# A two-layer decode kernel on one core: longer rows for some weights, a smaller last piece of wo, and the gate half of the last SwiGLU done ahead of the up half

## The chip, the cores and the metric

The kernel runs on one core of a Trainium2 chip. The core has five engines that run their own instruction streams: TensorE (PE in the profile, its weight loads PEld), VectorE (DVE), ScalarE (ACT), GpSimd (POOL) and SyncE (SP), which here only issues DMA transfers. All transfers of the core are split over 16 DMA engines. The metric is device time in microseconds; the time before is a median of several executions, and one more execution was profiled.

## The reference

Two equal layers, each an attention block on a cached window and a SwiGLU block, on a single token of width 640:

```python
W = min(4096, max(256, Sk // 4))            # 4096 of the 32768 cached rows
q = (x @ wq).reshape(B, Sq, 32, 192)        # wq: 640 x 6144
k = k_cache[:, :, Sk - W:, :]               # 32 heads, 4096 x 192 each
v = v_cache[:, :, Sk - W:, :]
p = softmax(q @ k^T * 192 ** -0.5)
att = (p @ v).reshape(B, Sq, 6144) @ wo     # wo: 6144 x 640
ffn = (silu(x @ w1) * (x @ w3)) @ w2        # w1, w3: 640 x 1536, w2: 1536 x 640

x = x + att(layernorm(x));  x = x + ffn(layernorm(x))    # layer 0
x = x + att(layernorm(x));  x = x + ffn(layernorm(x))    # layer 1
```

Both layers use the same weights and the same caches. Everything is bf16 in memory.

## The kernel before, in words

**Pages.** SBUF holds an arena of 16 slots (`NSLOT`), each 128 partitions by 6144 bf16 values (`PGW`), which is 1536 KB. One head's K window or V window fills one slot; so does one fifth of wq. wo comes as pieces of 9 chunks (a chunk is 128 rows of wo, 640 values on each partition), w1 and w3 as four of their five chunks of 1536 values, and a page `fc` holds the fifth chunk of w1, the fifth of w3 and the first four of the 12 chunks of w2. `fd` holds the next five chunks of w2. Three chunks of wo (`wo5`) and three of w2 (`keep`) stay in SBUF from layer 0 to layer 1, as do 14 heads of K (`RETAIN`); one of these is parked in PSUM (`stash`), so 13 slots are taken up around the change of layer and three are free.

**What sets the order.** `loads` (lines 163 to 198) is the list of all transfers in the order in which the data are used. `refill` (lines 200 to 212) takes from its head as long as a slot is free, and issues the transfers on SyncE; `done` frees a slot after its last use and calls `refill`. The instruction order on each engine is the order in which the Python code emits them, since nearly all are pinned by `pin`. The framework gives SyncE's transfers eight semaphores in turn: an issue waits for the landing of the transfer eight before it, and for the last reader of the slot that it overwrites. A transfer spreads over the 16 DMA engines by rows; each partition's row is one packet, 12288 B for a full page.

**One layer.** `attention` normalizes x, forms q (`qproj`: per wq chunk 12 products of 512 columns, then copies that lay q out as weights), and then runs over the 32 heads: for each K page two 32x32-block transposes on DVE (line 300), 12 score products, softmax per four heads, and six heads later 16 products with the V page. `wo_proj` (line 397) multiplies the chunks of wo in order, two products of 320 columns a chunk with a single column of weights, the three kept chunks last. `y_to_residual` adds the result to x, which lies spread over partitions in `xsq`.

**The ffn** (line 417). Layernorm gives `xs`. Four column strips of TensorE work side by side, so a chunk of w1 or w3 is four products of 384 columns: 16 for gate (page `fa`), 16 for up (`fb`), 4 and 4 for the fifth chunks (`fc`). Then both halves are copied to bf16, gate by ACT (line 444) and up by DVE (line 445), turned by three small products each to 12 values on each partition (line 449), and silu(gate) x up is made by one ACT and five DVE operations on 12 columns (lines 451 to 460), which give `htd`. In layer 0 twelve chunks of w2 are multiplied and added to the residual. In layer 1 `last_rows` (line 477) adds the residual by ten f32 product records (five products with the residual as weights; an f32 product has two records) into the same PSUM tile `f_ps`, then 48 products of `htd` with w2, four strips of 160 columns a chunk, the kept chunks seventh to ninth; DVE copies the row (line 489), and SyncE writes it out.

Layer 1's last transfers are split so that the last one is small: w2's chunks 4 to 8 come as 1280, 1280 and 640 columns.

Of the kernel before, what the change touches and what calls it, by code (L numbers as in the profile page):

```python
# [47 lines left out]
def kernel(  # L48
# [82 lines left out]
    zero = cst.tile([P, 32], BF16, name="zero")  # L131
# [15 lines left out]
    wq_v = A_wq.rearrange("(p c) n -> c p n", c=NCH)  # L147
# [5 lines left out]
    ORDER = ((3, 2, 1, 0), (1, 0, 2, 3))  # L153

# [7 lines left out]

    for layer in range(2):
        for c in range(NCH):
            loads.append((("q", layer, c), [(0, PGW, wq_v[c])]))
        for i in range(H + LEAD):
            for kind, g, cache in (("v", i - LEAD, A_v_cache), ("k", i, A_k_cache)):
# [3 lines left out]
                if kind == "k" and layer == 1 and h in RETAIN:  # L171
                    if h == STASH:
                        loads.append((("k", 1, h), []))
                    continue
                loads.append(((kind, layer, h),
                              [(0, PGW, cache[0, h, S0:SK, :].rearrange("(p t) d -> p (t d)", p=P))]))
        for w in range(6):
            parts = []
            for at, ci in enumerate(wo_order(layer)[9 * w:9 * w + 9]):
                blk, e = ORDER[layer][ci // 12], ci % 12  # L180
                if parts and parts[-1][2] == blk and parts[-1][3] + parts[-1][1] == e:
                    parts[-1][1] += 1
                else:
                    parts.append([at, 1, blk, e])
            parts = [(640 * at, 640 * n, wo_v[blk][:, 640 * e:640 * (e + n)]) for at, n, blk, e in parts]
            if w < 5:
                loads.append((("o", layer, w), parts))
            elif layer == 0:
                assert len(parts) == 1 and parts[0][1] == 1920
                loads.append((None, [(wo5[:], parts[0][2])]))  # L190
        loads.append((("fa", layer), [(0, PGW, w1_v[:, 0:PGW])]))
        loads.append((("fb", layer), [(0, PGW, w3_v[:, 0:PGW])]))
        loads.append((("fc", layer), [(0, 1536, w1_v[:, PGW:]), (1536, 1536, w3_v[:, PGW:]),
                                      (3072, 2560, w2_v[:, 0:2560])]))
        fd = [(0, 3200)] if layer == 0 else [(0, 1280), (1280, 1280), (2560, 640)]
        loads.append((("fd", layer), [(o, n, w2_v[:, 2560 + o:2560 + o + n]) for o, n in fd]))
        if layer == 0:
            loads.append((None, [(keep[:], w2_v[:, 5760:7680])]))

    def refill():  # L200
        while loads and (free or loads[0][0] is None):
            key, parts = loads.pop(0)
            if key is None:
                for dst, src in parts:
                    pin(nc.sync.dma_start(out=dst, in_=src))
                continue
            s = free.pop(0)
            home[key] = s
            for off, n, src in parts:
                pin(nc.sync.dma_start(out=arena[:, s * PGW + off:s * PGW + off + n], in_=src))  # L210
# [11 lines left out]
    def page(key):  # L222
        return arena[:, home[key] * PGW:home[key] * PGW + PGW]

    def done(key):
        free.append(home.pop(key))
        refill()
# [169 lines left out]
    def wo_proj(layer):  # L397
        y_ps = y_open("y_ps")
        for w in range(6):
            pg = page(("o", layer, w)) if w < 5 else wo5  # L400
            for cc, ci in enumerate(wo_order(layer)[9 * w:9 * w + 9]):
                n = 9 * w + cc
# [5 lines left out]
            if w < 5:  # L408
                done(("o", layer, w))
        y_to_residual(y_ps)  # L410

    def w2_chunk(layer, fcx):
        if fcx >= 9:
            return keep, 640 * (fcx - 9)
        return (page(("fc", layer)), 3072 + 640 * fcx) if fcx < 4 else (page(("fd", layer)), 640 * (fcx - 4))

    def ffn(layer):
# [15 lines left out]
        for ps, kind, c0, c1, off in ((g_ps, "fa", 0, 4, 0), (u_ps, "fb", 0, 4, 0),  # L433
                                      (g_ps, "fc", 4, 5, 0), (u_ps, "fc", 4, 5, 1536)):
            pg = page((kind, layer))
# [5 lines left out]
            if kind != "fc":  # L441
                done((kind, layer))
        gu = w20.rearrange("p (g n) -> p g n", g=2)
        pin(nc.scalar.copy(out=gu[:, 0, :], in_=g_ps[:, 0:384]))
        pin(nc.vector.tensor_copy(out=gu[:, 1, :], in_=u_ps[:, 0:384]))
        gt_ps = m_ps[:, 0:24].rearrange("p (g k j) -> p g k j", g=2, k=3)
        for gi in range(2):
            for k in range(3):
                mm(gt_ps[:, gi, k, :], lhsT=gu[:, gi, k:384:3], rhs=sel4[:], start=True, stop=True)
        ex = sml.tile([P, 12], F32, tag="ex", name="ex")  # L450
        pin(nc.scalar.activation(out=ex[:], in_=gt_ps[:, 0, :, :].rearrange("p k j -> p (k j)"), func=ACTF.Exp,
                                 scale=-1.0))
        ut = sml.tile([P, 12], F32, tag="ut", name="ut")
        pin(nc.vector.tensor_copy(out=ut[:], in_=gt_ps[:, 1, :, :].rearrange("p k j -> p (k j)")))
        gut = sml.tile([P, 12], F32, tag="gut", name="gut")
        pin(nc.vector.tensor_tensor(out=gut[:], in0=gt_ps[:, 0, :, :].rearrange("p k j -> p (k j)"), in1=ut[:],
                                    op=ALU.mult))
        pin(nc.vector.tensor_scalar_add(out=ex[:], in0=ex[:], scalar1=1.0))
        pin(nc.vector.reciprocal(out=ex[:], in_=ex[:]))
        pin(nc.vector.tensor_tensor(out=_ap(htd[:], 0, P, 0, [[1, 3], [3, 4]]),  # L460
                                    in0=gut[:].rearrange("p (k j) -> p k j", k=3),
# [100 lines left out]
```

## Time and profile before

| What | Value |
|---|---|
| Time, median of 3 runs | 528.83 us (528.5 to 529.74) |
| Profiled execution, its own time | 528.32 us |
| Span of its trace, first to last instruction | 526.6 us |
| Read from HBM | 221.58 MB, 421 GB/s over the span |
| PE busy | 275.0 us (52%), 2403 records |
| DVE busy | 256.4 us (49%) |
| ACT, POOL busy | 62.5 us, 16.2 us |
| Mean granted TensorE clock | 0.716 of full speed |

The page gives an engine's busy time as a share of the span, then the span in 40 slices with a digit for the busy tenths, the DMA queues, the chain of waits that ended last, and the costliest groups of instructions. In the timeline a row is a run of like instructions: start, length, engine, line, what is written and read, and in brackets the idle time before it with what ended it. The view by windows gives busy time and number of instructions for PE, PEld, DVE, ACT and POOL in each stretch, then the granted clock, the DMA share and GB/s. Every time in the text is counted from the span's start.

### The profile page before, as it was taken

To read this page: it belongs to the slowest core of one execution; us is meant where nothing else is said; L and a number is where in the kernel's file an instruction comes from. 1 tells how busy PE (TensorE), PEld (TensorE's weight loads), DVE (VectorE), ACT (ScalarE), POOL (GpSimd) and SP (SyncE) were. 2 spreads that over 40 slices of the span, in tenths; PEclk is the share of its full clock that TensorE was granted. 3 is DMA by queue.
4 is the path that set the end of the run, shared out by engine and by line. 5 is a ranking of instruction groups with operands and counts; after the bars stand their busy time and mean duration, and the time that the engine had idled before them with its cause. 6 is when DMAs were issued, how large, how long until landed. Compare 5 with 4: busy or idle time off the path is not lost.

```text
span 526.6 us, 5978 instructions
## 1 busy us (share of the span) xinstructions
PE 275.0 (52%) x2403; PEld 112.6 (21%) x2403; DVE 256.4 (49%) x393; ACT 62.5 (12%) x192; POOL 16.2 (3%) x74
## 2 busy tenths in 40 slices
PE   2344644472655644455545555687254756345455
PEld 1111211131222221122112112233022322112113
DVE  1199676556657475654002139531475645753001
ACT  1002020110102020112001002022111120202000
POOL 4000000000000000000000000000000000001000
PEclk9997968666756776586556558988677886686557
DMA  8999999999999999999999999999999999999995
GB/s 349 429 430 433 426 428 427 433 432 427 427 428 432 432 426 429 428 432 423 419 431 422 427 428 427 420 431 427 428 428 431 429 428 429 429 431 428 424 432 242
DMA packets 22355, 221.97 MB, mean 421 GB/s; under 512 B 2616, under 2 KB 2744, under 8 KB 5176
## 3 DMA queue, kind: packets, MB, share of 16 engines
q1 hardware_dynamic: 22184, 221.59, 99.3%
q8 instruction: 19, 0.31, 0.2%
q14 instruction: 8, 0.07, 0.0%
q10 hardware_dynamic: 144, 0.00, 0.0%
HBM read 221.58 MB, written 0.00 MB: 421 GB/s over the span
## 4 chain that ended last, share of the span: by engine, by line
DMA 85%; PE 7%; DVE 5%; issue 1%; ACT 1%; SPq 1%; DVEq 0%; ACTq 0%
DMA arena<-in_A_k_cache_dram 51%; DMA arena<-in_A_v_cache_dram 16%; DMA arena<-in_A_wo_dram 9%; DMA arena<-in_B_w_dram 6%; DMA arena<-in_A_wq_dram 3%; DVE arena L300 3%; PE s_ps L80 3%; PE o_ps L80 2%; PE y_ps L80 1%; SPq L210 1%; PE q_ps L80 1%; PE u_ps L80 0%; PE pss L80 0%; ACT w L337 0%; DVE t L322 0%
## 5 line engine op out<-in xcount | busy, mean ns | idle before, releaser
L80 PE MATMUL s_ps<-arena,wst 128*32 128x512 bf16 x768 | 153.7, 512 | 171.3 <-DVE arena L300 84.5
L300 DVE STREAM_TRANSPOSE arena<-arena 128x1536 uint32<-128x1536 uint32 x100 | 171.2, 1754 | 75.0 <-DMA arena<-in_A_k_cache_dram 74.6
L80 PE MATMUL o_ps<-arena,ptm 128*8 128x384 bf16 (+1 forms) x1024 | 113.5, 421 | 12.9 <-DMA arena<-in_A_v_cache_dram 12.9
L80 PEld LDWEIGHTS <-wst 128*32 128x32 bf16 x768 | 53.1, 115 | 256.2 <-issue 227.1
L80 PEld LDWEIGHTS <-ptm 128*8 128x8 bf16 (+1 forms) x1024 | 40.0, 99 | 49.9 <-issue 40.3
L332 ACT ACTIVATE tb<-m 32x16 f32<-32x16 f32 x16 | 3.4, 214 | 280.4 <-DVE m L329 280.4
L350 ACT COPY ptm<-w 32x64 bf16<-32x64 bf16 x80 | 23.6, 295 | 42.5 <-PE o_ps L80 39.3
L80 PE MATMUL y_ps<-arena,otd 128*1 128x320 bf16 x180 | 16.9, 459 | 15.1 <-DMA arena<-in_A_wo_dram 15.1
L80 PE MATMUL q_ps<-arena,xs 128*32 128x512 bf16 x120 | 14.5, 624 | 17.3 <-DMA arena<-in_A_wq_dram 14.7
L383 DVE SCALAR_TENSOR_TENSOR w<-pss,rl,mask 64x192 bf16<-64x192 f32 x16 | 6.7, 417 | 32.2 <-PE pss L80 32.2
L282 POOL COPY wst<-qt_sb 32x24 bf16<-32x24 bf16 x30 | 8.4, 281 | 432.7 <-PE s_ps L80 313.8
L340 DVE STREAM_TRANSPOSE w<-w 64x512 bf16<-64x512 bf16 x16 | 11.3, 705 | 14.4 <-ACT w L337 14.4
L248 DVE CAST w<-y_ps 128x320 bf16<-128x320 f32 x3 | 1.5, 490 | 34.4 <-PE y_ps L80 34.4
L322 DVE TENSOR_REDUCE t<-s_ps 64x1 f32<-64x512 f32 x16 | 10.6, 663 | 12.2 <-PE s_ps L80 12.1
L274 DVE CAST qt_sb<-pss 32x192 bf16<-32x192 f32 x2 | 0.7, 346 | 31.2 <-PE pss L80 31.2
L350 DVE COPY ptm<-w 32x64 bf16<-32x64 bf16 x48 | 9.9, 207 | 10.8 <-PE o_ps L80 9.6
L80 PEld LDWEIGHTS <-xs 128*32 128x32 bf16 x200 | 7.2, 119 | 35.7 <-issue 26.1
L355 DVE RECIPROCAL rl<-pss 64x1 f32<-64x1 f32 x16 | 2.6, 166 | 22.2 <-PE pss L80 22.2
L80 PEld LDWEIGHTS <-otd 128*1 128x1 bf16 x192 | 6.4, 103 | 25.8 <-issue 21.7
L337 ACT ACTIVATE w<-s_ps,nbt 64x512 bf16<-64x512 f32 x16 | 10.9, 682 | 5.6 <-DVE nbt L334 5.6
L376 ACT CAST w<-o_ps 128x384 bf16<-128x384 f32 x16 | 7.7, 479 | 33.0 <-PE o_ps L80 23.7
L80 PE MATMUL pss<-w,sel 128*64 128x192 bf16 x32 | 6.3, 286 | 9.5 <-ACT w L376 6.4
(82 smaller groups left out, 111.8 us busy)
## 6 DMA issues: line engine op xcount, KB each, us to landing
arena<-in_A_v_cache_dram SPq DMA_DIRECT2D x64, 1536.0 KB, 29.2
arena<-in_A_k_cache_dram SPq DMA_DIRECT2D x50, 1536.0 KB, 29.2
arena<-in_A_wq_dram SPq DMA_DIRECT2D x10, 1536.0 KB, 9.3
arena<-in_A_wo_dram SPq DMA_DIRECT2D x6, 1440.0 KB, 15.3
arena<-in_B_w_dram SPq DMA_DIRECT2D x4, 1536.0 KB, 11.1
arena<-in_A_wo_dram SPq DMA_DIRECT2D x4, 960.0 KB, 16.8
arena<-in_A_wo_dram SPq DMA_DIRECT2D x4, 480.0 KB, 21.8
arena<-in_B_w_dram SPq DMA_DIRECT2D x4, 384.0 KB, 14.6
```

The lines of the kernel that those rows point to most:

```text
L80: return pin(nc.tensor.matmul(*a, **k))
L210: pin(nc.sync.dma_start(out=arena[:, s * PGW + off:s * PGW + off + n], in_=src))
L282: pin((engs[a].copy if engs[a] is nc.scalar else engs[a].tensor_copy)(out=dst, in_=src))
L300: pin(nc.vector.transpose(x[:, w * sp:w * (sp + 1)].bitcast(U32), x[:, w * sp:w * (sp + 1)].bitcast(U32)))
L322: pin(nc.vector.reduce_max(out=t0[:, 0:1], in_=s_ps[0:64, :], axis=AX.X))
L332: pin(nc.scalar.mul(out=tb[32:64, :].rearrange("p (a z) -> p a z", a=4)[:, :, 0:HB], in_=mb, mul=-SCALE))
L337: pin(nc.scalar.activation(out=e[:], in_=s_ps[0:64, :], func=ACTF.Exp, bias=nbt[:, 0:1], scale=SCALE, accum_out=l[:]))
L340: pin(nc.vector.transpose(et[:], e[:]))
L350: pin((eng.copy if eng is nc.scalar else eng.tensor_copy)(out=dst, in_=src))
L355: pin(nc.vector.reciprocal(out=rl[half], in_=rl_ps[half]))
L376: pin(nc.scalar.copy(out=o_sb[:, 0:384], in_=o_ps[:, 0:384]))
L383: pin(nc.vector.scalar_tensor_tensor(out=om, in0=ot_ps[half], scalar=rl[half], in1=mask[half].unsqueeze(2).broadcast_to([64, 16, 12]), op0 ...
```

## The change

- wq of layer 0 comes as one chunk, two and two in place of five single ones; a pair takes two neighbouring slots.
- wo of layer 1 comes in pieces of 12, 12, 12 and 9 chunks in place of five of 9; a piece of 12 takes two neighbouring slots and is one transfer of 1920 KB. The piece of 9 is two transfers of 6 and 3 chunks (960 and 480 KB). The kept three chunks are multiplied before that last piece. Before, the pieces crossed head blocks and made seven transfers; now there are five.
- w1 of layer 1 comes whole, five chunks in two neighbouring slots; w3 as four chunks and one; w2's first nine chunks as 3840, 1280 and 640 columns. Six transfers in place of eight. The kept w2 chunks are multiplied first.
- The gate half is copied, turned and put through silu by the new `gate()`, and up is multiplied in by a single operation at the end; `gut` and one copy go. In layer 1 `gate()` is emitted between the products with w3's four chunks and those with its fifth, so DVE's copy of up now stands behind it. In layer 0 `gate()` stands after that copy.
- `refill` looks for the first free slot whose neighbours are free where a load has several keys, and stops otherwise; `zero` is 64 wide in place of 32.

```diff
+    def slots(key, width):
+        return [key] + [key + (i,) for i in range(1, -(-width // PGW))]
...
+    def wo_units(layer):
+        order = wo_order(layer)
+        step = 9 if layer == 0 else 12
+        return [order[at:min(at + step, 45)] for at in range(0, 45, step)] + [order[45:]]
...
-        for c in range(NCH):
-            loads.append((("q", layer, c), [(0, PGW, wq_v[c])]))
+        for c0, c1 in ((0, 1), (1, 3), (3, 5)) if layer == 0 else [(c, c + 1) for c in range(NCH)]:
+            loads.append(([("q", layer, c) for c in range(c0, c1)],
+                          [(0, PGW * (c1 - c0), wq_r[:, PGW * c0:PGW * c1])]))
...
+            if layer == 1 and w + 2 == len(units):
+                (at, n, blk, e), = parts
+                parts = [[at, n - 3, blk, e], [at + n - 3, 3, blk, e + n - 3]]
...
+        rows = 4 if layer == 0 else 5
+        loads.append((slots(("fa", layer), 1536 * rows), [(0, 1536 * rows, w1_v[:, 0:1536 * rows])]))
+        loads.append(([("fb", layer)], [(0, PGW, w3_v[:, 0:PGW])]))
...
+        else:
+            loads.append(([("fc", layer)], [(0, 1536, w3_v[:, PGW:])]))
+            loads.append(([("fd", layer)], [(o, n, w2_v[:, o:o + n]) for o, n in ((0, 3840), (3840, 1280), (5120, 640))]))
...
+            n = len(keys)
+            at = [s for s in free if all(s + i in free for i in range(n))]
+            if not at:
+                return
...
+        turns = list(range(len(units)))
+        if layer == 1:
+            turns[-2:] = turns[:-3:-1]
...
+        def turn(gi):
+            for k in range(3):
+                mm(gt_ps[:, gi, 4 * k:4 * k + 4], lhsT=gu[:, gi, k:384:3], rhs=sel4[:], start=True, stop=True)
+
+        def gate():
+            pin(nc.scalar.copy(out=gu[:, 0, :], in_=g_ps[:, 0:384]))
+            turn(0)
+            pin(nc.scalar.activation(out=ex[:], in_=gt_ps[:, 0, :], func=ACTF.Exp, scale=-1.0))
+            pin(nc.vector.tensor_scalar_add(out=ex[:], in0=ex[:], scalar1=1.0))
+            pin(nc.vector.reciprocal(out=ex[:], in_=ex[:]))
+            pin(nc.vector.tensor_tensor(out=ut[:], in0=gt_ps[:, 0, :], in1=ex[:], op=ALU.mult))
+
+        steps = ((g_ps, "fa", 0, 4, 0), (u_ps, "fb", 0, 4, 0), (g_ps, "fc", 4, 5, 0), (u_ps, "fc", 4, 5, 1536))
+        if layer == 1:
+            steps = ((g_ps, "fa", 0, 5, 0), (u_ps, "fb", 0, 4, 0), (u_ps, "fc", 4, 5, 0))
...
+            if layer == 1 and kind == "fb":
+                gate()
...
         pin(nc.vector.tensor_copy(out=gu[:, 1, :], in_=u_ps[:, 0:384]))
...
+        if layer == 0:
+            gate()
+        turn(1)
         pin(nc.vector.tensor_tensor(out=_ap(htd[:], 0, P, 0, [[1, 3], [3, 4]]),
-                                    in0=gut[:].rearrange("p (k j) -> p k j", k=3),
-                                    in1=ex[:].rearrange("p (k j) -> p k j", k=3), op=ALU.mult))
+                                    in0=gt_ps[:, 1, :].rearrange("p (k j) -> p k j", k=3),
+                                    in1=ut[:].rearrange("p (k j) -> p k j", k=3), op=ALU.mult))
...
-        for fcx in (0, 1, 2, 3, 9, 10, 11, 4, 5, 6, 7, 8):
+        for fcx in (9, 10, 11, 0, 1, 2, 3, 4, 5, 6, 7, 8):
```

## The prediction

> **What bounds the kernel now.** I read the page first: shares of time, DMA queues, the chain that ended last.
>
> ```profile
> span 526.6 us, 5978 instructions
> ...
> DMA  8999999999999999999999999999999999999995
> ...
> q1 hardware_dynamic: 22184, 221.59, 99.3%
> ...
> DMA 85%; PE 7%; DVE 5%; issue 1%; ACT 1%; SPq 1%; DVEq 0%; ACTq 0%
> ```
>
> The DMA row is full from the second slice to the last but one, one queue fills 99.3% of the engines' span, and 85% of the last chain is DMA. The stream of weights and cache pages is the bound; the other engines matter only where they starve it, and after its last byte. The change keeps the bytes (221.59 MB). So two questions remain: what a transfer costs beyond its bytes, and what follows the last bytes.
>
> For the first I read SyncE's rows in the timeline. Each issue waits for the landing of the transfer eight before it, so the distance of two rows is the distance of two landings:
>
> ```profile
> 430.40 0.33 SPq L210 DMA_DIRECT2D arena<-in_A_v_cache_dram  x1
> ...
> 445.04 0.33 SPq L210 DMA_DIRECT2D arena<-in_A_v_cache_dram  x1
> ...
> 496.64 0.33 SPq L210 DMA_DIRECT2D arena<-in_B_w_dram  x1
> 497.79 0.33 SPq L210 DMA_DIRECT2D arena<-in_B_w_dram  x1
> ```
>
> Four pages of 1536 KB lie between the first two rows shown, so one takes (445.04 - 430.40)/4 = 3.66 us. Between the last two rows a transfer of 480 KB landed: 1.15 us, where its bytes at the page's rate take 1.14.
>
> For the second I read the timeline of the end:
>
> ```profile
> 512.27 0.42 ACT L247 CAST w<-y_ps 128x320 bf16<-128x320 f32 x1 [17.03 <-PE y_ps L80]
> ...
> 515.64 1.56 PE L80 MATMUL g_ps<-arena,xs 128*32 128x384 bf16 x16 [1.31 <-DVE xs L242]
> ...
> 517.72 1.23 PE L80 MATMUL u_ps<-arena,xs 128*32 128x384 bf16 x14 [0.52 <-DMA arena<-in_B_w_dram]
> ...
> 520.75 0.24 PE L80 MATMUL pss<-sel,w 128*128 128x4 bf16 x3 [0.27 <-DVE w L445]
> ...
> 520.86 1.27 PE L80 MATMUL f_ps<-arena 128*128 128x32 f32 x10
> ...
> 522.23 0.45 PE L80 MATMUL f_ps<-arena,htd 128*1 128x160 bf16 x16
> ...
> 522.72 0.65 PE L80 MATMUL f_ps<-arena,htd 128*1 128x160 bf16 x20
> ...
> 523.41 0.32 DVE L489 CAST w<-f_ps 128x160 bf16<-128x160 f32 x1 [1.23 <-PE f_ps L80]
> 523.80 0.65 SPq L491 DMA_DIRECT2D out_dram<-w  x1
> ```
>
> The reader should see two races. The ten f32 products that add the residual (520.86 to 522.13) run beside the gate's small operations and end just before htd is ready (522.19): hidden by 0.06 us. And the 48 products with htd end at 523.39; their last four started at 523.12, since the last transfer's landing record stands at 523.08. Products and stream meet within about 0.1 us.
>
> Last, the busy time and granted clock in steps of 3.41 us, on which every change in the clock record falls:
>
> ```profile
> 511.28:514.70 3.42, 1.81 (x23) 0.93 (x12) 1.11 (x5) 0.42 (x1) 0.74 (x4) 0.50 0.98 419
> 514.70:518.11 3.41, 1.95 (x24) 0.67 (x28) 0.39 (x2) 0.41 (x2) 0.00 (x0) 0.50 0.99 406
> 518.11:521.52 3.41, 2.98 (x36) 1.62 (x29) 0.80 (x3) 0.66 (x2) 0.00 (x0) 1.00 0.86 343
> ...
> 279.18:282.59 3.41, 1.56 (x16) 0.47 (x16) 0.57 (x3) 0.41 (x2) 0.00 (x0) 0.50 0.96 406
> 282.59:286.00 3.41, 1.92 (x20) 0.82 (x21) 0.00 (x0) 0.48 (x1) 0.00 (x0) 0.50 1.04 423
> ```
>
> First number PE busy, last but two the clock. In the two ffn stages a step with 1.92 or 1.95 us of wide products was followed by full clock, one with 1.56 was not.
>
> **The change, part by part.** Times are in the profiled execution: 528.32 us, 1.7 of it outside the span of 526.6; the median of the runs, 528.83, is 0.51 above it.
>
> *Six transfers fewer* (two each in wq, wo, and w1/w2). Lower bound of one: 496.64 to 510.40 holds six landings with 5760 KB, 13.76 us against 5760/1536 x 3.66 = 13.73, so 0.03 for 2.25 extra transfers, 0.015 each. Upper bound: packet records are 460 ns for 12288 B, 149 for 3840 and 55 for 1280, a fit with 9 ns a packet; eight rows and one completion per engine make 0.08. I take 0.04, in the middle (the earliest of the 16 completions gives 0.04 too): 0.16 at wo's last landing (four gone), 0.24 at the end; bounds 0.1 and 0.5.
>
> *wq in 1+2+2 pages.* Chunk 3 waits for chunk 4, so 12 more products (1.3 us) follow the landing at 21.4. Scores and transposes start 1.3 us later. Nothing: the slot freed by the first k page is needed at 55.75, twenty us later, and all SyncE rows to 140 wait for landings alone. Without that cover it would cost up to 1.3.
>
> *Pages of two slots* (three of wo, one of w1) must wait for two neighbouring slots. By the built order they wait for v and k products that ran at 457.7, 468.1 and 475.4 to 476.0, and w1's for one at 478.3; their turns by landings are 467.0, 470.6, 474.3 and 485.9. One is 1.8 us late, with seven transfers (some 25 us) queued ahead. Nothing; it costs only beyond that. Layer 1's start, where slots are scarce, is unchanged.
>
> *Layer 0's gate* loses two DVE copies of 0.17 and starts its exponential before the up half; its w2 lands later than that. Nothing gained.
>
> *Nothing in time*: the zero tile twice as wide and one small tile less (the arena keeps its address; the memset runs at the start, beside the first landing), kept w2 chunks first (they are in SBUF since layer 0), and POOL's copies for the f32 products, which follow the residual and so come 1.2 us earlier, seven us ahead of their use.
>
> *wo's end.* The last landing now brings 3 chunks, 6 products in place of 24 (18 waiting and 6 kept). Landing 510.34 - 0.16 = 510.18; two groups of four at 0.27 apart and 0.47 for the last: done at 510.96 (before: 512.16). With 3.49 from there to the first gate product, it could start at 514.45. But w1 is one transfer of 1920 KB: 4.57 after wo, 514.75. Of 1.2 us gained, 0.3 is waited away.
>
> *Gate.* 20 products from 514.79 (four cost 0.32): 516.7. w3's four chunks land at 518.41; PE idles 1.7. Its 16 products let the next start at about 519.75; three turning products 0.24, then exponential, add, reciprocal, product in a row (0.19, 0.16, 0.23, 0.17, gaps 0.03 each): 520.9. Only then, in DVE's order, the up copy that stood first before: 0.56, 521.5. Behind it on DVE waits the last product; for it waits PE: up's turn 521.55 to 521.8, and, behind that in PE's order, **the ten f32 products, from 521.65**. The gate after the turn is one DVE operation (0.20), so htd is there at 522.0, and the cover of the ten is gone. At full clock (0.11 apart) they let the 48 start at 522.76, which end at 523.75: +0.36. The stream's last landing, 518.41 + 0.91 + 2.29 + 0.76 + 0.38 = 522.75, no longer decides.
>
> *The clock.* Before, gate and up products stood 0.5 us apart and filled a step. Now 1.9 us of gate, 1.7 idle, then 1.5 of up. Few positions of a step hold 1.9 busy before 521.6, and where the gate alone releases it, the thin step behind (up at full clock is under 1 us) can lose it again. At half clock the ten cost more: the layernorm's f32 pair at 513.73 takes 0.60 for two of 0.38, 0.22 apart, so +1.1; the 48, by the y row (320 columns, 0.27 per four), are 0.133 per four of 160 instead of 0.068: +0.7. Bounds: 0 and +1.8. Moving the step's position over one period, with release between 1.45 and 1.75 us of dense columns, I get +0.6 on average. I take +0.55: sum 0.36 + 0.55 = **+0.9**.
>
> The Trainium skill, TensorE: Matmul & The Clock Gate, Part 1 (The HAM clock gate), has full clock only after a sustained busy window of some 3.4 us, the window running free of the program. The rows above agree on the length, but 57% busy was enough. By the rule as it stands both groups would be at half clock: +2.2 instead of +0.9.
>
> **The rivals.** The forecast, late gate and f32 products at partly half clock, +0.4 to +1.5: 58%.
> - *Half clock to the end*: 0.36 + 1.1 + 0.7 = +2.2, 531.0. For it: 1.7 us idle. Against: up and the ten may fill a step by 521.6. It is slower once release comes after 522.5. 16%.
> - *Full clock in time*: +0.36, 529.2. 13%.
> - *The stream still sets the end*, the gate chain being some 0.7 us shorter than I make it: -0.24 to -0.5, 528.5. For it: products and stream met before. Against: DVE's order. 8%.
> - *A transfer costs far more than its bytes*, over 0.3 us each, some of it in the engines' lag (first and last completion of one transfer are 3.1 us apart at the end): 527.0 or less. Against: the rows at 496.64. 5%. The Trainium skill, DMA: Bandwidth & Descriptors, Anatomy of one DMA, fits 2.0 us fixed per transfer, which would be 12 us for six; the row of 1.15 us for 480 KB contradicts it as a cost of the stream.
>
> **How the numbers follow.** 528.83 + 0.9 = 529.7. A measurement tells about 0.2% (1.06 us) from no change. Slower: the half clock (16%) and some two fifths of the forecast (24%): 40%. Same: the rest of the forecast (34%), the full clock (13%), most of the stream's case (6%): 53%. Faster: the last rival and the edge of the stream's case, 7%. Range: 528.4 leaves out the last rival and half of the stream's case (9%), 531.0 half of the half-clock case and a long forecast (10%).
>
> **What would show it.** Right: SyncE's rows 3.66 apart as before; up's cast behind the gate's three DVE rows; ten f32 products after 521.3 with the htd products right behind them and not behind DVE; a clock below 1 there. Wrong: htd products waiting for DMA (stream's case), pages landing faster, or the ten done before htd.

## The result and the profile after

The changed kernel takes 529.54 us (median of 14 runs, 528.87 to 531.43), the kernel before beside it 528.92 (14 runs, 528.23 to 529.9): ratio 1.0019, 95% interval 1.001 to 1.0027. That is 1.0 us slower (0.5 to 1.4; the medians are 0.62 apart), just inside the 0.2% that the prediction called no change. The forecast was 529.7.

The profiled execution of the changed kernel took 531.0 us, a span of 529.2: one of the longer ones, 1.5 over the median. That of before was 0.5 under its median. The two profiles thus show the mechanism larger than the medians do.

The page of the changed kernel, DMA queue and shares of the last chain:

```profile
span 529.2 us, 5964 instructions
...
q1 hardware_dynamic: 21320, 221.59, 98.7%
...
DMA 85%; PE 8%; DVE 5%; issue 1%; ACT 0%; SPq 0%; DVEq 0%; ACTq 0%
```

The bytes are the same, with 864 packets fewer, but the queue fills 98.7% of a longer span in place of 99.3%: the stream isn't slower, what follows it is longer. PE has one point more of the chain, DMA no more. The packet records say the same: added up over the queue and divided by the 16 engines they give 522.72 us before and 522.45 after.

Where it goes is in the chain that ended last (start, us, what), its end:

```profile
518.79 1.57 PE u_ps L80 x11
...
521.33 0.17 DVE ut L482
521.50 0.47 DVE w L498
...
522.03 0.24 PE pss L80 x3
522.27 3.91 PE f_ps L80 x52
...
526.20 0.33 DVE w L531
```

Before, the last 48 products took 1.16 us, directly behind htd at 522.19. Now up's cast stands behind the gate's product, up's turn behind the cast, and 3.91 us of products behind the turn. The timeline of the changed kernel says which:

```profile
515.19 1.91 PE L80 MATMUL g_ps<-arena,xs 128*32 128x384 bf16 x20 [1.74 <-DMA arena<-in_B_w_dram]
...
518.79 1.58 PE L80 MATMUL u_ps<-arena,xs 128*32 128x384 bf16 x16 [1.69 <-DMA arena<-in_B_w_dram]
...
521.42 0.55 DVE L498 CAST w<-u_ps 128x384 bf16<-128x384 f32 x1
...
522.13 2.32 PE L80 MATMUL f_ps<-arena 128*128 128x32 f32 x10
522.31 0.19 DVE L502 TENSOR_TENSOR htd<-pss,ut 128x12 bf16<-128x12 f32 x1 [0.34 <-PE pss L80]
524.38 0.57 PE L80 MATMUL f_ps<-keep,htd 128*1 128x160 bf16 x12
524.73 1.42 PE L80 MATMUL f_ps<-arena,htd 128*1 128x160 bf16 x36
```

htd is ready at 522.50, 0.3 later than before. The ten f32 records, 520.86 to 522.13 before, now start at 522.13 and take 2.32 us; the 48 products start at 524.38 and take 1.80. The last landing stands at 523.16 (523.08 before): those products don't wait for it any more. The end of the products moves from 523.39 to 526.18: 2.15 us by their start, 0.64 by their own length. (Before, 0.13 of the 1.16 us was a wait for the last landing: the last four products started 0.198 us behind the four ahead of them, the other groups of four 0.069.)

Both lengths are the clock. The end of the changed kernel in the steps on which its own clock record falls (they stand elsewhere than before), PE busy first and the clock last but two:

```profile
513.13:516.55 3.42, 1.68 (x20) 0.99 (x22) 0.69 (x3) 0.41 (x2) 0.36 (x2) 0.50 1.00 423
516.55:519.96 3.41, 1.72 (x24) 0.48 (x16) 0.00 (x0) 0.48 (x1) 0.00 (x0) 0.50 0.98 407
519.96:523.37 3.41, 2.38 (x22) 1.62 (x17) 1.23 (x5) 0.18 (x1) 0.00 (x0) 0.50 0.42 166
```

The granted clock is 0.50 from 482.41 to the end, where before it went up at 518.11. f32 records stand 0.213 us apart (0.112 before), groups of four of the last products 0.133 (0.069). The step with 1.72 us, all of it gate's and up's products, was not followed by full clock; the one with 2.38 was not either, but only some 0.9 of that are up's products, the rest turns and f32 records. In the profile of the kernel called "gate late" below, a step with 1.76 us of gate's and up's products, 516.19 to 519.60, was followed by full clock. Two steps so alike with different outcomes leave much to where a step happens to fall; they are two profiles and give no threshold.

### The profile page after: what moved, and what is told of

Same layout as the page of the kernel before. It is cut to its first block, busy times and chain, and to the rows that moved or that the text cites. A ratio compares the mean times of both kernels' runs of the same rounds, so it can differ in the third digit from the quotient of the medians.

```text
span 529.2 us, 5964 instructions
## 1 busy us (share of the span) xinstructions
PE 278.9 (53%) x2403; PEld 114.0 (22%) x2403; DVE 255.8 (48%) x391; ACT 62.5 (12%) x192; POOL 16.1 (3%) x74
## 3 DMA queue, kind: packets, MB, share of 16 engines
q1 hardware_dynamic: 21320, 221.59, 98.7%
## 4 chain that ended last, share of the span: by engine, by line
DMA 85%; PE 8%; DVE 5%; issue 1%; ACT 0%; SPq 0%; DVEq 0%; ACTq 0%
DMA arena<-in_A_k_cache_dram 51%; DMA arena<-in_A_v_cache_dram 17%; DMA arena<-in_B_w_dram 7%; DMA arena<-in_A_wq_dram 7%; DVE arena L325 4%; DMA arena<-in_A_wo_dram 3%; PE s_ps L80 3%; PE o_ps L80 2%; PE y_ps L80 1%; PE f_ps L80 1%; PE q_ps L80 1%; PE u_ps L80 0%; PE pss L80 0%; DVE w L498 0%; SPq L234 0%
## 5 line engine op out<-in xcount | busy, mean ns | idle before, releaser
L80 PE MATMUL s_ps<-arena,wst 128*32 128x512 bf16 x768 | 156.0, 521 | 166.4 <-DVE arena L325 84.3
L80 PE MATMUL y_ps<-arena,otd 128*1 128x320 bf16 x180 | 15.7, 461 | 14.7 <-DMA arena<-in_A_wo_dram 14.7
```

The costliest lines, as they stand in the source:

```text
L80: return pin(nc.tensor.matmul(*a, **k))
```

## The experiments

Three theories. **A**, of the prediction: up's turn comes late behind VectorE's gate operations, so that the ten f32 records lose their cover, and the idle time between gate and up costs the clock. **B**: longer rows and pages of two slots slow or starve the stream. **C**: w3's later landing behind w1's fifth chunk sets the end, wherever the f32 records stand. A fourth, **F**, came up on the way. Ratios are to the kernel before, with the 95% interval:

| kernel | ratio | interval |
|---|---|---|
| the change | 1.0019 | 1.001 to 1.0027 |
| f32 products early | 0.9995 | 0.9986 to 1.0003 |
| idle filled, two places | 1.0021 | 1.0012 to 1.003 |
| idle filled, one place | 1.0006 | 0.9995 to 1.0017 |
| wq and wo alone | 1.001 | 1.0 to 1.002 |
| wq and wo, f32 early | 1.0004 | 0.9995 to 1.0013 |
| before, f32 early | 1.0009 | 1.0 to 1.0018 |
| ffn part alone | 1.0033 | 1.002 to 1.0045 |
| f32 early, up's cast on ScalarE | 1.0011 | 1.0003 to 1.002 |
| f32 early, up's cast on ScalarE, VectorE shifted | 1.0108 | 1.0095 to 1.0122 |
| ffn part alone, VectorE shifted | 1.0133 | 1.012 to 1.0147 |
| gate late | 1.0014 | 1.0005 to 1.0023 |
| before, V pages split | 1.0034 | 1.0021 to 1.0046 |

**f32 products early.** The change with one move, into a bank of its own:

```diff
-            ident = (ident, xw)
+            f_ps = pss[:, 0:512]
+            for c in range(NCH):
+                mm(f_ps[:, c:160:NCH], lhsT=xw[:, 128 * c:128 * c + 128], rhs=ident, start=(c == 0), stop=False)
         g_ps = ps_a.tile([P, 512], F32, tag="a", name="g_ps")
```

> The changed kernel with one move: the five f32 residual products are issued before the gate's products, into a PSUM bank of their own; the stream, the order of the transfers and the gate are untouched. Theory A (the ten f32 records stand behind up's turn in TensorE's order, nothing covers them, and at half clock they cost twice): the records move to about 514, beside the wait for w1's page; the htd products wait for VectorE's last product and then for the last landing. In the changed kernel's trace the last product could start at 522.50 instead of 524.38, so the end moves by -1.0 to -1.9 us where the clock is low, and the median by about -0.4 to -1.2: 528.4 to 529.2, ratio to the kernel before 0.999 to 1.0005. Theory B (longer rows or pages of two slots slow the stream): the stream is the same, so the ratio stays at 1.002. Theory C (w3 comes one chunk later behind w1's long transfer, and this sets the end): the ratio stays within 0.0005 of 1.002, as w3 comes no earlier.

528.71 us, ratio 0.9995: the loss is gone. Timeline of this kernel:

```profile
513.54 1.44 PE L80 MATMUL pss<-arena 128*128 128x32 f32 x10 [0.35 <-POOL arena L463]
...
522.31 0.19 DVE L504 TENSOR_TENSOR htd<-pss,ut 128x12 bf16<-128x12 f32 x1 [0.33 <-PE pss L80]
522.56 0.38 PE L80 MATMUL pss<-keep,htd 128*1 128x160 bf16 x12 [0.28 <-DVE htd L504]
522.76 0.80 PE L80 MATMUL pss<-arena,htd 128*1 128x160 bf16 x36
```

w1 and w3 land at 515.05 and 518.76 (515.05 and 518.75 in the changed kernel), the cast and htd come at the same times to 0.01, the last landing at 523.16 in both. Only the ten records are elsewhere, at 513.54, beside the wait for w1; the 48 products start right behind htd and end at 523.59. The intervals of the two ratios don't meet. That shows A's first half, and refutes B and C as the cause: long rows, two-slot pages and w3's place are all still in it. The clock was up here from 517.94 to 524.77, past the last product; whether by the move or by where its steps fell one profile can't say, so the 1.3 us between 1.0019 and 0.9995 are both parts of A together.

**Idle time filled.** The change with wide products into a bank that nothing reads, to hold the clock up:

```diff
+            if layer == 1 and kind != "fb":
+                for d in range(24 if kind == "fa" else 8):
+                    j = d % 4
+                    mm(pss[32 * j:32 * j + 32, 512:896], lhsT=xs[:, 0, 3:35],
+                       rhs=_ap(page(("fa", 1)), 0, P, 3 * j, [[12, 128], [1, 3]]),
+                       start=True, stop=True, tile_position=(0, 32 * j))
             if layer == 1 and kind == "fb":
                 gate()
```

> The changed kernel with idle TensorE time filled: 24 more wide products behind the gate's twenty and 8 behind up's fifth chunk, into a PSUM bank that nothing reads; the order of everything else, the transfers and the late f32 records stay. It isolates the clock. If half of the loss is the clock (theory A's +0.55 of +0.9 on average, up to +1.8), the granted clock is 1.00 from about 518.4 on, the ten f32 records stand 0.11 apart as before and the 48 last products 0.017 each, and the end comes near the forecast's full-clock case: +0.2 to +0.6 over the kernel before, ratio 1.0003 to 1.0012. Theory B or C: the clock is no part of it, ratio stays at 1.002.

530.14 us, ratio 1.0021, not the 1.0003 to 1.0012 expected. The clock did come up, 1.00 from 519.75 to 526.58 in its trace, but the second group of products stood in the way (timeline, PE alone):

```profile
522.02 0.87 PE L80 MATMUL pss<-arena,xs 128*32 128x384 bf16 x8 [0.56 <-DVE ut L482]
522.82 0.24 PE L80 MATMUL pss<-sel,w 128*128 128x4 bf16 x3
```

They waited for VectorE's product ut, which reads the same PSUM tile, and up's turn then waited behind them; its cast had been done at 522.43, so they cost 0.4 us; taken off, that leaves 1.0013, still inside the interval of the change. I had taken them to run beside the cast. A second version leaves them out and has twenty products behind the gate's:

```diff
-            if layer == 1 and kind != "fb":
-                for d in range(24 if kind == "fa" else 8):
+            if layer == 1 and kind == "fa":
+                for d in range(20):
```

> The changed kernel with twenty wide products into a bank that nothing reads behind the gate's twenty, and none behind up's fifth chunk, where they had held up the gate's second turn by some 0.4 us. Theory A with the clock as about half of the loss: the late f32 records stay, but the clock is up when they come, so the median is 0.3 to 0.8 us under that of the first filled version (530.14) and 0 to 0.6 under the changed kernel's: ratio to the kernel before 1.0005 to 1.0017. If the clock is no part of the loss, the ratio stays at 1.002.

529.42 us, ratio 1.0006, inside what was expected; but the interval overlaps that of the change, so the clock's share is 0.7 us by the two ratios and anything from nothing to 1.7 by their intervals; that it has one is not shown. Its steps of the clock (PE busy first, clock last but two) show how short-lived the gain is:

```profile
516.55:519.96 3.41, 3.41 (x45) 1.80 (x38) 0.00 (x0) 0.48 (x1) 0.00 (x0) 0.50 1.00 417
519.96:523.37 3.41, 2.38 (x28) 1.42 (x20) 1.22 (x5) 0.18 (x1) 0.00 (x0) 1.00 0.48 186
523.37:526.79 3.42, 2.01 (x50) 1.60 (x49) 0.33 (x1) 0.00 (x0) 0.00 (x0) 0.50 0.00 0
```

One full step released the clock; behind the step with the gate's small operations it was lost again, though PE is listed as busy for 2.38 us of that step, and the 48 products ran at half clock, 1.80 us. The prediction had this case, "the thin step behind can lose it again".

**wq and wo alone** (the ffn part of the diff taken back):

```diff
-        rows = 4 if layer == 0 else 5
+        rows = 4
-        steps = ((g_ps, "fa", 0, 4, 0), (u_ps, "fb", 0, 4, 0), (g_ps, "fc", 4, 5, 0), (u_ps, "fc", 4, 5, 1536))
-        if layer == 1:
-            steps = ((g_ps, "fa", 0, 5, 0), (u_ps, "fb", 0, 4, 0), (u_ps, "fc", 4, 5, 0))
-        for ps, kind, c0, c1, off in steps:
+        for ps, kind, c0, c1, off in ((g_ps, "fa", 0, 4, 0), (u_ps, "fb", 0, 4, 0),
+                                      (g_ps, "fc", 4, 5, 0), (u_ps, "fc", 4, 5, 1536)):
...
```

> Only wq in longer rows and wo in longer rows with its small last transfer (four transfers fewer); layer 1's w1, w3, w2 and the gate as before. Theory A: the end's order is as before, wo's end comes 0.16 us earlier by four transfers at 0.04, and the residual is done some 1.2 us earlier, where w1's page is not there yet: -0.1 to -0.5, ratio 0.999 to 0.9998, and the ten f32 records stand beside the gate's small operations. Theory B: the longer rows are in it, so it is slower by +0.3 to +1.0 us, ratio 1.0005 to 1.002. Theory C: as A.

529.37 us, ratio 1.001, with 1.0 as its lower bound: at best the same, where A and C had a small gain. That is B's number, but hardly B's cause: the f32 products early, with the same rows in them, were at 0.9995. Its timeline:

```profile
515.60 1.55 PE L80 MATMUL g_ps<-arena,xs 128*32 128x384 bf16 x16 [1.32 <-DVE xs L265]
519.14 1.57 PE L80 MATMUL u_ps<-arena,xs 128*32 128x384 bf16 x16 [1.99 <-DMA arena<-in_B_w_dram]
...
522.26 1.61 PE L80 MATMUL f_ps<-arena 128*128 128x32 f32 x10
```

The gate's products stand where they stood before, at 515.60, but the stream is late in this execution: up's start at 519.14 in place of 517.72. Measured against the stream, the gate is done earlier, and TensorE idles 1.99 us before up, 0.52 in the kernel before. The clock is 0.50 from 516.14 to 522.97, and the ten f32 records take 1.61 us in place of 1.27; the products with htd start at 523.80, where htd was ready at 523.58. So a stage that is done early in front of its landing went with a lower clock; but with the last landing at 524.38, which alone would let the products end at 524.7, the late f32 records cost no more than some 0.1 us of this execution. To tell the two apart, the same kernel with the f32 products early:

```diff
-            ident = (ident, xw)
+            f_ps = pss[:, 0:512]
+            for c in range(NCH):
+                mm(f_ps[:, c:160:NCH], lhsT=xw[:, 128 * c:128 * c + 128], rhs=ident, start=(c == 0), stop=False)
```

> wq and wo of the change, ffn as before, and the f32 residual products early. Without that move it came out at 1.001, where a gain of 0.16 us had been expected. Its trace has the gate's products 1.5 us ahead of up's, as the residual is done earlier, so that TensorE idles 2.0 us before up in place of 0.5, and half clock at the ten f32 records (1.61 us in place of 1.27), which end 0.1 us after htd is due; but also a last landing 1.3 us later than in the kernel before. If the loss is the clock at the f32 records, the ratio goes back to 0.9993 to 1.0003; if it lies in the stream (layer 1's start, where pages wait for slots), it stays at 1.0007 or more.

529.13 us, ratio 1.0004 with 0.9995 to 1.0013: between the two answers, and its interval overlaps that of 1.001. In its trace the products end with the stream (last landing 523.33, last product 523.6). How much of the 1.001 is the f32 records and how much the stream, and whether there is a loss at all, stays open.

**The kernel before with the f32 products early:**

```diff
-            ident = (ident, xw)
+            f_ps = pss[:, 0:512]
+            for c in range(NCH):
+                mm(f_ps[:, c:160:NCH], lhsT=xw[:, 128 * c:128 * c + 128], rhs=ident, start=(c == 0), stop=False)
```

> The kernel before with the one move: the five f32 residual products ahead of the gate's products, in a bank of their own. In the profiled execution they were hidden by 0.06 us at full clock, and the last landing set the end: no gain there. Where the clock is low at the end they take twice as long and push the htd products. So it is the same or a little faster, ratio 0.999 to 1.0. Against the changed kernel with the same move (0.9995) it says what the rest of the change is worth without the late f32 products: by theory A -0.24 us for six transfers fewer at the most, so this one is between the same and 0.0005 above that.

529.36 us, ratio 1.0009: a miss. In the kernel before nobody waits for w1 at that place, and at half clock the ten records are in the gate's way:

```profile
515.66 2.31 PE L80 MATMUL pss<-arena 128*128 128x32 f32 x10 [0.35 <-DVE st L234]
517.90 1.57 PE L80 MATMUL g_ps<-arena,xs 128*32 128x384 bf16 x16
```

The layernorm was done at 516.57 and w1 was there; the gate starts 1.3 us after that. htd is ready at 523.66, and the 48 products end at 524.73, where behind the last landing (524.08) alone they could have ended at 524.4. The same move that gains 1.3 us in the changed kernel loses some 0.5 here by the ratio (nothing to 0.95 by its interval), 0.3 in this trace: the changed kernel has a wait for w1 to put it in, this one has none.

**The ffn part alone** (wq and wo as before):

```diff
-        for c0, c1 in ((0, 1), (1, 3), (3, 5)) if layer == 0 else [(c, c + 1) for c in range(NCH)]:
+        for c0, c1 in [(c, c + 1) for c in range(NCH)]:
-        step = 9 if layer == 0 else 12
+        step = 9
...
```

> Only layer 1's part of the change: w1 as one transfer of five chunks in two slots, w3's fifth chunk and w2 regrouped (two transfers fewer), half of the gate done after the up half's first four chunks; wq and wo as before. Theory A: the late f32 records are in it, so it is slower as the whole change is, +0.4 to +1.5 us, ratio 1.001 to 1.003; the gate's products start later than in the changed kernel (wo's last landing brings 24 products again), some 515.7, so the idle time before up is shorter and the clock may stay a step longer. Theory B: without the long rows of wq and wo it is within +0.3 of the kernel before, ratio up to 1.0006. Theory C: slower, as under A.

530.48 us, ratio 1.0033, above what A gave. Timeline of the end:

```profile
522.32 1.27 PE L80 MATMUL f_ps<-arena 128*128 128x32 f32 x10
...
523.73 0.80 PE L80 MATMUL f_ps<-arena,htd 128*1 128x160 bf16 x36
```

This is the prediction's full-clock case: idle before up 1.03 us, clock 1.00 from 518.45, records 0.11 apart. The products end at 524.55, 1.2 after the last landing (523.37), against 0.3 before. That much is A. The rest is behind it: the output, issued at 524.96, landed at 527.45, 2.49 us later, where before it took 1.66 (523.80 to 525.46). The DMA view of the last five us has one packet that is not there in the kernel with the f32 products early:

```profile
q8 instruction: 1, 0.02, 1.2%
q14 instruction: 1, 0.01, 0.6%
q1 hardware_dynamic: 8, 0.00, 0.1%
```

The q14 packet, 8192 B of instructions, starts at 526.07 and takes 0.49 us; three of the output's four rows move by 526.26, the fourth at 526.55. Each profile has such a packet: at 527.25 before, behind the output; at 522.70 in the changed kernel, ahead of it. The q8 packet, 16384 B, is not it: in the kernel before one ran from 523.23 to 524.15 and the output still took 1.66. Theory **F**: where the q14 packet falls on the output it costs 0.83 us. The late row is 0.3 of that; what makes the rest the packets don't show. Without that, 530.48 would be 529.65, the changed kernel's time.

**f32 early, up's cast on ScalarE:**

```diff
-        pin(nc.vector.tensor_copy(out=gu[:, 1, :], in_=u_ps[:, 0:384]))
+        pin((nc.scalar.copy if layer == 1 else nc.vector.tensor_copy)(out=gu[:, 1, :], in_=u_ps[:, 0:384]))
```

> The changed kernel with the f32 residual products early, and the up half's cast on ScalarE in layer 1, so that it doesn't wait behind the gate's three VectorE operations. In the trace of the version with the f32 products early alone, up's products were done at about 520.95 and VectorE's cast ran from 521.43 to 521.98; on ScalarE it can start at once, htd comes some 0.4 us earlier (522.1), and the 48 last products then wait for the last landing (523.16) alone: 0 to 0.4 us under that version, ratio 0.9988 to 0.9998. If the stream sets the end in most executions of that version already, no difference to it.

529.36 us, ratio 1.0011, slower than with the cast on VectorE by 0.65. htd came 0.27 earlier (522.23), and the chain of this kernel has only the stream and four products at its end, as expected:

```profile
507.27 16.08 DMA arena<-in_B_w_dram
523.35 0.04 issue
523.39 0.27 PE pss L80 x4
523.66 0.02 issue
523.69 0.32 DVE w L529
```

So nothing before the output explains it. The output does: issued at 524.07, landed at 526.56, 2.49 us, with the q14 packet at 525.21. In all other profiles of this document the output takes 1.64 to 1.67 us, and the packet lies elsewhere. Two kernels to test F, each of the two hit ones with VectorE's instructions moved four places on:

```diff
     nc.vector.memset(onesb[:], 1.0)
+    spare_v = cst.tile([P, 4], F32, name="spare_v")
+    for i in range(4):
+        nc.vector.memset(spare_v[:, i:i + 1], 0.0)
```

> The version with f32 early and up's cast on ScalarE (1.0011), with four small VectorE memsets more at the start, into a tile that nothing reads: VectorE's instructions stand four places further. Theory F (a fetch of 8192 B of instructions falls on the output's transfer): in that version's trace an instruction packet of 8192 B starts at 525.21, 1.2 us after the last cast and in the middle of the output's transfer, which takes 2.49 us from issue to landing; with the cast on VectorE it started at 522.74 and the output took 1.66. Four places further the fetch comes with an earlier instruction, the output takes 1.66 again, and the median falls by about 0.8: 528.4 to 528.8, ratio 0.999 to 1.0. Theory G (the cast on ScalarE is itself slower, or the difference is spread between executions): ratio stays at 1.0005 to 1.0015.

> Layer 1's ffn part alone (1.0033), with four small VectorE memsets more at the start into a tile that nothing reads. Theory F: in that part's trace the instruction packet starts at 526.07, on the output's transfer, which takes 2.49 us; shifted, it takes 1.66, so the median falls from 530.5 by about 0.8, to some 529.4 to 529.9, ratio 1.001 to 1.002: what is left is the late f32 records, as in the whole change. Theory G: ratio stays at 1.0025 or more.

534.63 and 535.84 us, 1.0108 and 1.0133: over 5 us slower, in place of 0.8 faster. Yet F's part came as expected. The q14 packet moved to 528.68 and 529.25, ahead of the output (issued at 530.31 and 531.67), and the output took 1.66 us in both; from the last landing to the end of the span it is 3.3 us in place of 4.2, and 4.2 in place of 5.1. What went wrong is the stream. The page of the unshifted and of the shifted kernel with the cast on ScalarE:

```profile
DMA packets 21492, 221.97 MB, mean 421 GB/s; under 512 B 2520, under 2 KB 2648, under 8 KB 4568
```

```profile
DMA packets 21492, 221.97 MB, mean 417 GB/s; under 512 B 2520, under 2 KB 2648, under 8 KB 4568
```

Same packets, same bytes, slower. In the built programs the tile of 16 bytes moves the arena from byte 24064 of each partition to 24096, and most packets take longer (medians: 12288 B 460 to 464 ns, 7680 B 291 to 295, 3072 B 121 to 125; the mean of 12288 B rises by 5.6). Those of 24576, 2560 and 1280 B don't, by their medians (912, 102 and 55 ns). Added up and divided by 16 engines the packets come to 528.70 us in place of 522.47, 6.2 more, while the median rose by 5.3; for the ffn part it is 6.4 and 5.4. The 1.0 that is missing both times (0.96 and 1.05) is about what F gives back (0.83). F thus fits every trace, and the medians, but isn't isolated: a run with the fetch moved and the arena in place was not made. Nor was one with the arena moved alone, so that its address slows the stream is argued and not shown.

**Gate late.** The change with layer 1's gate behind up's fifth chunk:

```diff
-            if layer == 1 and kind == "fb":
-                gate()
         pin(nc.vector.tensor_copy(out=gu[:, 1, :], in_=u_ps[:, 0:384]))
-        if layer == 0:
-            gate()
+        gate()
         turn(1)
```

> The changed kernel with layer 1's gate after up's fifth chunk, as in layer 0: VectorE casts up first, then the gate's add, reciprocal and product; transfers and the place of the f32 records behind up's turn unchanged. From the changed kernel's trace: up's products done at 520.99, so its cast runs to 521.55 in place of 521.97, up's turn and the f32 records start 0.4 us earlier, and htd comes at about the same time (522.4). Theory A: as the f32 records set the end, it is 0.4 us faster than the changed kernel, ratio 1.0005 to 1.0015. If the early gate saves time, it is slower than the changed kernel, 1.002 or more.

529.71 us, ratio 1.0014: the number is inside what was expected, the reason isn't. Up's cast did start as soon as up was done, but nothing behind it came earlier:

```profile
521.54 0.56 DVE L496 CAST w<-u_ps 128x384 bf16<-128x384 f32 x1 [6.05 <-PE u_ps L80]
...
522.77 0.22 PE L80 MATMUL pss<-sel,w 128*128 128x4 bf16 x3 [1.11 <-DVE ut L482]
```

Up's turn waits for ut here, since it writes the tile that ut reads. From up's first product to the first f32 record it is 3.29 us, in the changed kernel 3.34. But this profile had full clock from 519.60 on, and up's twenty products took 1.90 us in place of 2.19; from their end to the first f32 record it is 1.39 here and 1.15 in the changed kernel. So doing half of the gate early shortened that stretch by some 0.2 us, too little for the medians to show. The f32 records lost the gate's small operations as their cover in both.

**A transfer by itself.** The kernel before with every second V page as two transfers:

```diff
-                loads.append(((kind, layer, h),
-                              [(0, PGW, cache[0, h, S0:SK, :].rearrange("(p t) d -> p (t d)", p=P))]))
+                src = cache[0, h, S0:SK, :].rearrange("(p t) d -> p (t d)", p=P)
+                cut = ((0, PGW // 2), (PGW // 2, PGW // 2)) if kind == "v" and i % 2 == 0 else ((0, PGW),)
+                loads.append(((kind, layer, h), [(o, n, src[:, o:o + n]) for o, n in cut]))
```

> The kernel before with every second of layer 0's and layer 1's V pages as two transfers of half rows (6144 B rows in place of 12288): the same bytes, 32 transfers more. By the price taken for a transfer, 0.04 us, the last landing comes 1.3 us later: ratio 1.0024 (bounds 0.015 and 0.08: 1.0009 and 1.0048). With a price of over 0.3 us each (a rival) it is 9.6 us or more, ratio 1.018; by the Trainium skill's 2.0 us fixed per transfer (DMA: Bandwidth & Descriptors, Anatomy of one DMA), if it were paid in a row, 64 us.

530.73 us, ratio 1.0034: 32 transfers more cost 1.8 us (1.1 to 2.4), 0.056 each (0.035 to 0.076). Its packets add up to 524.89 us against 522.72, 0.068 for each transfer. By the medians it is 0.073: half a row takes 234 ns, two of them 8 more than the 460 of a whole row, eight rows to an engine, and 9 ns for one completion more. The six transfers of the change are then worth 0.2 to 0.45 us; its own packets add up to 0.27 less.

The Trainium skill, DMA: Bandwidth & Descriptors, Anatomy of one DMA — SWDGE (gpsimd) path, fits 2.0 us fixed per transfer, for transfers that GpSimd issues; the prediction left that condition out. Here SyncE issues them, and what one more costs in a queue that always has the next transfer behind the last is 0.056 us, with its interval far below 2.0.

## Why the prediction was right

529.7 was forecast, 529.54 came: the forecast's case, +0.4 to +1.5, with the cause that it named, the ten f32 records late behind up's turn. That it came within 0.2 us is in part luck: single executions of the changed kernel lie between 528.87 and 531.43, the gain that the sum took from the stream did not show, and the clock's +0.55 is an average over cases of which any one execution has one. Point by point:

- *Six transfers fewer* at 0.04: 0.24 in all, 0.27 by the packets of the two profiles, 0.2 to 0.45 by the split V pages. The size fits, though packets of one and the same stream add up to 522.39 to 523.05 in six profiles. It did not come out as an earlier end: the prediction had 522.75 for the last landing, of the six profiles with the change's stream and the arena in its old place five have 523.16 to 523.38 and one 523.99. The sum started from an execution whose last landing, 523.08, was an early one; another with the same stream (f32 early on the kernel before) had 524.08. The gain is smaller than that spread.
- *wq in 1+2+2, pages of two slots*: nothing, and none is seen. With both in it and the f32 products early, the time is that of before (0.9995, 0.9986 to 1.0003).
- *Layer 0's gate and the small items*: in the same kernel at 0.9995, and not isolated by any run.
- *wo's end* and *gate*: y done, w1's landing, gate, w3's landing each came 0.3 to 0.4 us after the forecast's time, as the stream did; the differences between them were right to 0.1: gate 1.91 us for 1.9, idle 1.69 for 1.7.
- *Up's cast behind VectorE's three rows, f32 records behind up's turn*: right in order; forecast at 521.65, measured at 522.13, 0.34 of the difference from the stream, and the rest fits up at half clock.
- *The clock*: its share of the median is not settled. The profiled execution is the rival's (half clock to the end), and its two terms were +1.05 and +0.64 where +1.1 and +0.7 had been worked out; the ffn part alone and the gate late were profiled at full clock. How many of the changed kernel's executions had which, the times alone don't say.
- *"Layer 1's start, where slots are scarce, is unchanged"*: the program there is unchanged, but its time isn't fixed, as the last section shows. It isn't what put this stream 0.3 to 0.4 us behind the forecast: the kernel with the f32 products early, whose page there was issued early (318.65), had the landings of w1, w3 and the last transfer at the same times to 0.01. That delay stays unexplained.

The Trainium skill, TensorE: Matmul & The Clock Gate, HAM oscillation — how this bites in real kernels, warns of bursts of products with waits for DMA of over 3.4 us between them, where the clock falls back every time. This trace is a milder case: 1.91 us of products, 1.69 of waiting, 1.58 of products, and a clock that was at 0.50 already and did not come up. A clock that falls back is seen in the kernel with one place filled, at 523.37, behind a step with 2.38 us busy and so without any wait of 3.4.

## What to carry to other kernels

A small group of instructions that is free where it stands is free because of a particular piece of idle time: when you reorder the work around it, ask what idle time covers it now, and move it into a wait for data that exists in the new order (here 1.3 us), not into one that exists only on paper (the same move cost 0.5 in the kernel before by the ratio, nothing to 0.95 by its interval). Finishing a stage early in front of a landing that doesn't move gained nothing here; in two profiles it went with a clock that stayed down, which is a risk to look at and not a cost that was shown. And where differences of a tenth of a per cent are at stake, look at the end of the program and at the addresses of the big buffers, before explaining them by the edit: a 16-byte tile that nothing reads came with 5 us.

No version here beats both kernels: the change with the f32 products early (0.9995, 0.9986 to 1.0003) beats the change and can't be told from the kernel before.

## What the runs showed of the hardware

- With the destination moved by 32 bytes (24064 to 24096, a multiple of 256 to one of 32), packets of 3072 to 15360 B took 2 to 4 ns longer by their medians, those of 12288 B 4 (5.6 in the mean), and the kernel 5.3 us, 1.0% of its time. The Trainium skill, DMA: Bandwidth & Descriptors, How a descriptor splits into AXI transactions, splits a descriptor into transactions of 256 B that start on multiples of 256 B; worked out from that, as an estimate, 12288 B take 48, and 49 from an address 32 B past a multiple (the Trainium skill speaks there of what is read, and not of the destination). A small cost that hardly depends on the size agrees with that; that rows of 24576, 2560 and 1280 B got no longer by their medians does not, nor does it explain why instruction fetches of 16384 B, whose destination the profile doesn't name, went from 0.94 to 1.07 us. No run here moved the arena by 256 or alone.
- Instruction fetches go through the same DMA engines. They take 19 packets of 16384 B (q8) in each execution, some 0.93 us of one engine each (1.07 in the two shifted kernels). In the kernel before, the first and the last completion of one transfer drift apart from 0.3 us at the start to 3.1 at the end; whether the fetches do it wasn't tested. One packet of 8192 B on the output went with 0.83 us more, in two profiles of two.
- At layer 1's start pages are issued when a slot comes free, some 2 to 3 us ahead of their turn, and slots come free with the score products. TensorE's score products ahead of such an issue, in the kernel before and in the changed one:

```profile
316.91 2.05 PE L80 MATMUL s_ps<-arena,wst 128*32 128x512 bf16 x12 [0.91 <-DVE arena L300]
```

```profile
316.78 2.74 PE L80 MATMUL s_ps<-arena,wst 128*32 128x512 bf16 x12 [0.91 <-DVE arena L325]
```

  The clock went up at 316.72 in the one and at 321.99 in the other, the page was issued at 318.45 and at 319.52, and by the page whose first completion stands at 350.94 before the stream of the changed kernel was 0.5 us (first completion) to 0.8 us (last) behind. Of the nine other profiles with V pages whole and the arena in its old place, three had the clock up by 317.1 and the page issued by 318.80; six had it up from 320.3 or later and the page issued at 319.55 to 320.04. The kernel before, with nothing changed but the f32 products at its end, is among the late ones: it goes with where the clock's steps fall in an execution, not with the change. What it costs at the end is open. Of the seven late ones three have their last landing at 523.99 to 524.38; the other four have it at 523.16 to 523.38, where the four early ones, at 523.08 to 523.37, have it too.
